# New fixed orders of TensorE, ScalarE and VectorE work in a fused attention and channel-mix kernel

## The chip, the core and the metric

The kernel runs on one core of a Trainium2 chip. The metric is the device time of one execution in microseconds (us). Five engines work side by side, each through its own list of instructions and strictly in the order of that list: TensorE (PE: matmuls and transposes; PEld is its weight loads), ScalarE (ACT), VectorE (DVE), GpSimd (POOL) and SyncE (SP). The last two mostly issue transfers (DMAs) here.

## The reference

Eight batches of eight heads; a sequence of 576 positions, 64 numbers per head. Sliding-window attention with a bias that grows with distance, and then a channel mix with a shift by one position:

```python
scores = scale * np.matmul(q, k.transpose(0, 1, 3, 2))
bias = slopes[:, None, None] * (-np.abs(rel).astype(np.float32))[None, :, :]
mask = (rel >= 0) & (rel < window)           # window = 128
...
x_prev = np.concatenate([np.zeros((B, 1, D), dtype=np.float32), x[:, :-1, :]], axis=1)
xk = mu_k * x + (1.0 - mu_k) * x_prev
xr = mu_r * x + (1.0 - mu_r) * x_prev
k = np.maximum(xk @ w_k, 0.0)
v = k * k @ w_v
r = 1.0 / (1.0 + np.exp(-(xr @ w_r)))
return (r * v).astype(np.float32)
```

Here x is the attention's output, with all heads of a position side by side (512 numbers); w_k is 512 x 1024, w_v 1024 x 512, w_r 512 x 512.

## The kernel before, in words

**Attention.** A batch is worked in four pairs of heads (g = 0 to 3). For a pair, q and k come as rows of positions and are transposed on TensorE (lines 1249 and 1252 for the first half of batch 0, line 1173 for its second half and for batches 1 and 2, line 911 for batch 3) or by transposing DMAs (batches 4 to 7); ScalarE or VectorE copies them from PSUM to tiles qk (line 759). Scores are matmuls of 64 rows, two heads at a time (line 789), ahead of which batch 0's first half gets its bias by a matmul (line 773). ScalarE takes the exponential into tiles at (line 806), VectorE multiplies by a mask (lines 815 to 827), TensorE multiplies by V, which has a column of ones (line 855, tiles vs, and tv for the last 64 positions). VectorE takes the reciprocal of the sums (line 861) and scales (line 867, tiles xu). xu is transposed to xt on TensorE (lines 894 and 911, copies on line 759) or by DMA. VectorE forms the shifted difference (line 954) and the two mixes xk and xr (line 961).

**Masks and tails.** The mask is made at the start: matmuls of line 1197, exponentials on ScalarE (line 1202), copies on VectorE (line 1215). The last 64 positions of q and k ("tails", tiles ts and tt) are transposed on lines 1015 (batch 0) and 986.

**Channel mix.** Pieces of 256, 512 and 384 positions. Eight groups of four matmuls by w_k (line 1078), each followed by a ReLU on ScalarE (line 1085) and a square on ScalarE or VectorE (lines 1057 and 1059, tiles rl to kk); per 128 positions one group by w_r (line 1096) with a tanh on ScalarE (line 1103), and two groups by w_v (line 1112). VectorE multiplies both into the output (line 1117), which SP stores (line 1142).

**Warm-up.** TensorE begins with matmuls whose result nobody reads (line 750); there are 56 of them.

**What sets the order.** Every step is a node of a plan. A table `ORDER` holds, for PE, ACT and DVE, the numbers of the nodes in the order in which that engine is to do them. A node that two engines can do (`copy_any`, `square`) is done by the engine in whose list its number stands. `Plan.run` goes through the table, follows the dependences, takes PSUM banks (eight, named p1) and tiles as they come free, and so gives each engine its list. POOL's list of loads is in the order of the code; SP's list follows from the plan. On the chip an engine waits at its next instruction until what that needs is there, and nothing behind it overtakes it (TensorE's weight loads excepted). Loads on POOL are held to eight in flight: the ninth issue waits until the first has landed.

Of the kernel before, what the change touches and what calls it, by code (L numbers as in the profile page):

```python
# [23 lines left out]
85 75 68 56 41 43 71 62 90 40 78 44 69 72 45 52 74 88 61 64 39 76 83 67 86 53 93 91 57 59 81 51 73 70 54 48 63  # L24
50 58 84 87 42 105 47 65 94 55 49 80 103 117 60 77 79 95 89 46 92 82 119 66 120 106 97 141 129 122 108 143 144
131 37 132 125 146 111 196 179 134 149 157 162 137 213 199 165 182 168 185 202 239 236 216 219 230 245 188 242
251 171 222 205 191 248 174 233 225 312 300 259 254 208 315 345 303 298 333 318 306 256 261 336 348 339 257 293
273 276 351 270 264 309 321 279 262 267 441 324 342 285 282 354 453 486 288 439 295 357 456 489 296 290 459 492
291 474 414 387 378 477 480 372 369 390 408 495 426 551 395 405 420 366 375 384 483 381 400 444 447 498 397 462
398 565 583 568 423 411 402 450 403 434 556 465 597 417 429 436 392 588 600 559 393 431 591 437 562 432 571 519  # L30
525 522 507 603 574 513 510 724 697 727 536 531 594 528 516 546 700 688 606 541 538 548 539 715 691 718 549 627
669 660 624 694 633 630 639 543 654 703 621 721 675 544 644 663 706 822 730 615 618 533 810 825 733 534 657 636
672 649 666 641 786 789 683 642 798 813 801 754 646 763 792 651 647 742 816 745 757 678 652 804 748 828 751 760
685 943 919 907 686 781 931 910 768 773 946 934 766 680 778 783 949 771 779 769 784 776 681 846 876 891 888 913
774 882 885 849 858 863 937 897 837 922 1023 834 894 879 840 1011 1026 873 843 925 868 855 1035 999 1014 852 902
860 870 865 1038 1002 866 1029 861 955 871 1017 961 964 1041 904 976 958 1005 973 984 970 994 899 967 900 905
979 989 981 1086 1101 1107 1098 1089 1053 1092 982 1050 1104 1056 1095 1047 1068 1065 986 1062 1059 1110 996 987
# [1387 lines left out]
```

## Time and profile before

| | |
|---|---|
| median of 3 runs | 231.36 us (230.56 to 231.84) |
| the profiled execution | 231.85 us, of which its span is 228.2 |
| instructions | 6317, of which 2517 matmuls |
| mean granted clock of TensorE | 0.985 |
| last matmul's end, span's end | 224.9 us, 228.2 us |

A row of a timeline reads: start, length, engine, line, operation, tile written<-tiles read, shapes, how many instructions were merged into the row and, in brackets, how long the engine stood idle before it and what ended that. Lengths of matmuls overlap, so the pace of a group is the distance from its start to the next group's start. A row of a table by stretches reads: stretch, its length, busy time (and instructions) of PE, PEld, DVE, ACT and POOL, granted clock of TensorE (1.00 is full speed), busy share of the DMA engines, GB/s.

### The profile page before, as it was taken

To read this page: it belongs to the slowest core of one execution; us is meant where nothing else is said; L and a number is where in the kernel's file an instruction comes from. 1 tells how busy PE (TensorE), PEld (TensorE's weight loads), DVE (VectorE), ACT (ScalarE), POOL (GpSimd) and SP (SyncE) were. 2 spreads that over 40 slices of the span, in tenths; PEclk is the share of its full clock that TensorE was granted. 3 is DMA by queue.
4 is the path that set the end of the run, shared out by engine and by line. 5 is a ranking of instruction groups with operands and counts; after the bars stand their busy time and mean duration, and the time that the engine had idled before them with its cause. 6 is when DMAs were issued, how large, how long until landed. Compare 5 with 4: busy or idle time off the path is not lost.

```text
span 228.2 us, 6317 instructions
## 1 busy us (share of the span) xinstructions
PE 219.5 (96%) x2517; PEld 128.7 (56%) x2517; DVE 188.5 (83%) x431; ACT 153.3 (67%) x274; POOL 92.1 (40%) x118
## 2 busy tenths in 40 slices
PE   8989889999998999999999999999999999999994
PEld 8656645845656455556665555446564554664442
DVE  6788999898768999999898978699989999854243
ACT  2897899898989875987488834933598532646111
POOL 8765557599960983347585534400000000000000
PEclk9976999999999999999999999999999999999999
DMA  6999999999999999999999999999951162120225
GB/s 166 177 187 203 193 192 179 196 181 150 182 172 151 123 170 155 194 144 159 156 193 159 171 117 184 127 233 144 261 136 30 59 138 59 47 95 0 92 92 184
DMA packets 132492, 33.96 MB, mean 149 GB/s; under 512 B 119784, under 2 KB 127984, under 8 KB 132464
## 3 DMA queue, kind: packets, MB, share of 16 engines
q0 software_dynamic: 95728, 16.26, 96.7%
q1 hardware_dynamic: 34992, 16.72, 37.5%
q10 hardware_dynamic: 1744, 0.59, 1.1%
q8 instruction: 19, 0.31, 0.5%
q14 instruction: 9, 0.07, 0.1%
HBM read 33.56 MB, written 9.44 MB: 188 GB/s over the span
## 4 chain that ended last, share of the span: by engine, by line
PE 85%; ACT 7%; DMA 3%; POOL 2%; issue 1%; DVE 0%; DVEq 0%; POOLq 0%; ACTq 0%
PE ps L1078 28%; PE ps L1112 26%; PE ps L1096 14%; PE ps L855 7%; PE ps L789 7%; DMA qx<-in_k_dram 3%; ACT qk L759 3%; ACT at L806 2%; PE ps L911 1%; ACT xt L759 1%; ACT rl L1085 1%; POOL vs L563 1%; PE ps L1173 1%; POOL qx L559 0%; PE ps L1015 0%
## 5 line engine op out<-in xcount | busy, mean ns | idle before, releaser
L1078 PE MATMUL ps<-xk,wk_sb 128*128 128x256 bf16 (+2 forms) x416 | 72.6, 318 | 0.3 <-ACT at L806 0.3
L1085 ACT ACTIVATE rl<-ps 128x256 bf16<-128x256 f32 (+2 forms) x104 | 46.9, 475 | 38.4 <-PE ps L1078 30.9
L1112 PE MATMUL ps<-wv_sb,kk 128*128 128x512 bf16 (+2 forms) x296 | 70.1, 374 | 0.0
L806 ACT ACTIVATE at<-ps 128x1024 bf16<-128x1024 f32 (+2 forms) x68 | 63.4, 987 | 5.0 <-PE ps L789 4.0
L1078 PEld LDWEIGHTS <-wk_sb 128*128 128x128 bf16 x416 | 38.4, 99 | 23.8 <-ACT rl L1085 1.2
L1112 PEld LDWEIGHTS <-kk 128*128 128x128 bf16 x296 | 26.6, 98 | 29.7 <-ACT rs L1103 1.0
L827 DVE TENSOR_TENSOR at<-at,mask 128x1024 bf16<-128x1024 bf16 x56 | 37.4, 683 | 3.3 <-ACT at L806 3.2
L563 POOL DMA_DIRECT2D vs<-in_v_dram x32 | 28.4, 895 | 24.5 <-PE ps L855 15.8
L1059 DVE TENSOR_TENSOR kk<-rl 128x256 bf16<-128x256 bf16 (+2 forms) x93 | 30.1, 335 | 8.5 <-ACT rl L1085 8.5
L1096 PE MATMUL ps<-wr_sb,xr 128*128 128x512 bf16 x144 | 36.4, 380 | 0.0
L1103 ACT ACTIVATE rs<-ps 128x512 bf16<-128x512 f32 x36 | 21.6, 612 | 21.7 <-PE ps L1096 21.7
L1117 DVE SCALAR_TENSOR_TENSOR ot<-rs,ps 128x512 f32<-128x512 bf16 (+2 forms) x37 | 24.2, 660 | 10.3 <-PE ps L1112 10.2
L867 DVE TENSOR_TENSOR xu<-ps,rc 128x640 bf16<-128x640 f32 (+2 forms) x36 | 26.5, 742 | 0.3
L961 DVE SCALAR_TENSOR_TENSOR xr<-dl,mu_sb,xt 128x576 bf16<-128x576 bf16 (+1 forms) x32 | 24.8, 777 | 0.0
L855 PEld LDWEIGHTS <-at 128*128 128x128 bf16 x576 | 21.3, 97 | 6.2 <-ACT qk L759 1.1
L961 DVE SCALAR_TENSOR_TENSOR xk<-dl,mu_sb,xt 128x576 bf16<-128x576 bf16 (+1 forms) x32 | 24.5, 777 | 0.1
L855 PE MATMUL ps<-vs,at 128*128 128x65 bf16 x512 | 22.1, 193 | 0.6 <-ACT qk L759 0.6
L594 POOL DMA_DIRECT2D cb<-in_k_dram x20 | 17.7, 908 | 9.7 <-DMA vs<-in_v_dram 6.8
L1096 PEld LDWEIGHTS <-xr 128*128 128x128 bf16 x144 | 13.0, 98 | 14.2 <-ACT rl L1085 0.7
L594 POOL DMA_DIRECT2D cb<-in_q_dram x20 | 17.7, 905 | 5.0 <-PE ps L1078 1.4
L759 ACT COPY qk<-ps 128x512 bf16<-128x512 bf16 (+1 forms) x27 | 13.6, 552 | 2.6 <-PE ps L1252 2.2
L861 DVE RECIPROCAL rc<-ps 128x10 f32<-128x10 f32 (+2 forms) x36 | 7.4, 208 | 8.9 <-PE ps L855 7.4
(83 smaller groups left out, 188.8 us busy)
## 6 DMA issues: line engine op xcount, KB each, us to landing
out_dram<-ot SPq DMA_DIRECT2D x35, 256.0 KB, 3.8
vs<-in_v_dram POOLq DMA_DIRECT2D x32, 128.0 KB, 9.0
cb<-in_q_dram POOLq DMA_DIRECT2D x20, 128.0 KB, 9.7
cb<-in_k_dram POOLq DMA_DIRECT2D x20, 128.0 KB, 7.5
wk_sb<-in_moe_w_k_dram POOLq DMA_DIRECT2D x2, 512.0 KB, 9.2
cb<-in_q_dram POOLq DMA_DIRECT2D x4, 256.0 KB, 10.0
cb<-in_k_dram POOLq DMA_DIRECT2D x4, 256.0 KB, 9.9
wv_sb<-in_moe_w_v_dram POOLq DMA_DIRECT2D x2, 512.0 KB, 11.0
```

Source lines behind the costliest of these rows:

```text
L563: return dma(POOL, 256, issue_t(1024), lambda e: nc.gpsimd.dma_start(out=vs_buf[h.idx][:, j, :, 0:D], in_=v[b, :, 128 * j:128 * j + 128].r ...
L594: return [dma(POOL, 256, issue_t(1024), lambda e, r=r: nc.gpsimd.dma_start(out=cb_buf[h.idx][:, i, r], in_=src[:, :, r]), [g], kind="q") f ...
L806: lambda e, ah=ah, w=w, hp=hp: nc.scalar.activation(out=ah(), in_=two(hp)[:, :, 0:w], func=AF.Exp, scale=float(scale)), (), [hp])
L827: nc.vector.tensor_tensor(out=a, in0=a, in1=m, op=ALU.mult)
L855: nc.tensor.matmul(a[:, hl, t - t0], lhsT=at[:, lo:lo + 128], rhs=vs[:, u, 2 * g + hl, 0:W] if u < NF else tvb[:, 2 * g + hl, 0:W], start= ...
L867: nc.vector.tensor_tensor(out=out_, in0=a5()[:, :, :, 0:D], in1=rc[:, :, 0:nt, None].to_broadcast([128, 2, nt, D]), op=ALU.mult)
L961: lambda e: nc.vector.scalar_tensor_tensor(out=buf[hk.idx][:, g, e0 + c0:e0 + c1], in0=dls(), scalar=mu[:, g:g + 1], in1=xc(1), op0=ALU.mu ...
L1059: nc.vector.tensor_tensor(out=out, in0=in_, in1=in_, op=ALU.mult)
L1078: nc.tensor.matmul(one(hp)[:, 0:n], lhsT=wk_sb[:, po, 128 * fo:128 * fo + 128], rhs=xk_buf[hx.idx][:, po, c0:c1], start=(po == 0), stop=(p ...
L1085: a = op(ACT, act_t(n), [s], pr, lambda e, hp=hp, hr=hr: nc.scalar.activation(out=rl_buf[hr.idx][:, 0:n], in_=one(hp)[:, 0:n], func=AF.Rel ...
L1096: nc.tensor.matmul(one(hp), lhsT=xr_buf[hx.idx][:, po, 128 * c:128 * c + 128], rhs=wr_sb[:, po], start=(po == 0), stop=(po == NPO - 1))
L1112: nc.tensor.matmul(one(hv)[:, a:b], lhsT=kk_buf[hk.idx][:, fo, o:o + 128], rhs=wv_sb[:, fo, a:b], start=(fo == 0), stop=(fo == NFO - 1))
```

## The change

Only the three lists in `ORDER` differ. All nodes, their code, the number of matmuls and the loads on POOL with their order are the same. The core of the diff, one line of PE's list:

```diff
 ORDER = {
     "PE": [int(x) for x in """
...
-85 75 68 56 41 43 71 62 90 40 78 44 69 72 45 52 74 88 61 64 39 76 83 67 86 53 93 91 57 59 81 51 73 70 54 48 63
...
+49 58 52 60 42 70 68 87 57 44 86 39 67 84 88 79 73 62 83 40 64 61 53 91 43 56 59 69 41 90 93 82 65 74 72 47 95
```

Sixteen nodes change their engine: nine go from VectorE to ScalarE, seven the other way (twelve of them squares, four copies). Of the warm-up matmuls 36 stay at TensorE's head, 4 stand among its first attention work, and 16 between the transposes and scores of batch 0's second half. Counted over TensorE's whole list, a 64-row matmul follows a 128-row one or the other way round 98 times, where it was 78 times. SP stores some outputs earlier or later among its transposing DMAs.

ScalarE at its start, before (after its four loads; L1202 makes a mask, qk are the transposed q and k, at the exponentials, xt the transposed output):

```order
L759 ACT_TABLE_LOAD
L759 COPY qk_72<-ps 128x2x256
L1202 ACTIVATE mask<-ps 128x4x256
L806 ACTIVATE at_77<-ps 128x2x384
L806 ACTIVATE at_78<-ps 128x2x384
L1202 ACTIVATE mask<-ps 128x4x256
L759 CAST qk_74<-ps 128x2x256
```

and now:

```order
L1202 ACT_TABLE_LOAD
L1202 ACTIVATE mask<-ps 128x4x256
L759 COPY qk_71<-ps 128x2x256
L759 COPY qk_72<-ps 128x2x256
L806 ACTIVATE at_77<-ps 128x2x384
L806 ACTIVATE at_78<-ps 128x2x384
L1202 ACTIVATE mask<-ps 128x4x256
L759 CAST qk_74<-ps 128x2x256
```

The first mask goes ahead of the first copy, and a second copy, which VectorE did, comes behind it.

TensorE where batch 0's first half is transposed (xu are the scaled outputs, at the exponentials, warm the warm-up tile), as a piece of the difference:

```order
+L894 LDWEIGHTS xu_86
+L894 MATMUL ps<-ident,xu_86 128x128
+L894 LDWEIGHTS xu_86
+L894 MATMUL ps<-ident,xu_86 128x128
+L750 LDWEIGHTS warm
+L750 MATMUL ps<-warm 128x128
 L894 LDWEIGHTS xu_85
 L894 MATMUL ps<-ident,xu_85 128x128
 L894 LDWEIGHTS xu_85
 L894 MATMUL ps<-ident,xu_85 128x128
-L855 LDWEIGHTS at_77
-L855 MATMUL ps<-vs_63,at_77 128x65
```

A warm-up matmul stands between two pairs of transposes, and the attention matmuls that stood behind the second pair have moved.

TensorE at the scores of batch 2's first two pairs of heads (tiles qk_72 and qk_73), before:

```order
L789 MATMUL ps<-qk_72 128x256
L789 LDWEIGHTS qk_72
L789 MATMUL ps<-qk_72 128x256
L789 LDWEIGHTS qk_73
L789 MATMUL ps<-qk_73 128x256
```

and now:

```order
L789 MATMUL ps<-qk_72 128x256
L789 LDWEIGHTS qk_72
L789 MATMUL ps<-qk_72 128x256
L911 LDWEIGHTS xu_85
L911 MATMUL ps<-ident,xu_85 128x64
```

The second pair's scores no longer follow the first's: twenty transposes of xu, four of the tails and two groups of w_v matmuls stand between them.

82 rows, old and new, of the table ORDER are left out of this document.

## The prediction

> **What bounds the kernel now.** I read the page first: its busy shares, its slices with the granted clock, and its chain.
>
> ```profile
> PE 219.5 (96%) x2517; PEld 128.7 (56%) x2517; DVE 188.5 (83%) x431; ACT 153.3 (67%) x274; POOL 92.1 (40%) x118
> PE   8989889999998999999999999999999999999994
> PEclk9976999999999999999999999999999999999999
> PE 85%; ACT 7%; DMA 3%; POOL 2%; issue 1%; DVE 0%; DVEq 0%; POOLq 0%; ACTq 0%
> ```
>
> TensorE carries 85% of the chain. A new order can't remove matmuls, so it can only win time in which TensorE waits, runs at a lower clock, or changes its mode. The table by stretches says where such time is (columns: PE, PEld, DVE, ACT, POOL busy, clock, DMA):
>
> ```profile
> 0.00:4.50 4.50, 3.51 (x34) 3.51 (x35) 2.52 (x21) 1.28 (x1) 3.54 (x10) 1.00 0.54 149
> 11.30:14.70 3.40, 2.70 (x104) 1.94 (x100) 2.45 (x13) 3.00 (x9) 2.70 (x4) 1.00 1.47 196
> 14.70:18.10 3.40, 2.80 (x48) 1.72 (x46) 3.40 (x13) 3.40 (x9) 1.40 (x3) 0.50 1.80 185
> 18.10:21.50 3.40, 3.23 (x22) 2.12 (x23) 2.97 (x11) 2.51 (x7) 2.15 (x4) 0.50 1.25 205
> 25.00:34.00 9.00, 7.34 (x184) 4.30 (x182) 8.54 (x21) 8.66 (x20) 5.52 (x7) 1.00 1.54 193
> 40.00:50.00 10.00, 9.47 (x248) 6.84 (x245) 9.22 (x20) 9.39 (x25) 7.48 (x10) 1.00 2.00 193
> 50.00:80.00 30.00, 29.40 (x393) 16.95 (x392) 24.93 (x52) 26.68 (x47) 21.81 (x27) 1.00 1.93 155
> 80.00:224.90 144.90, 144.88 (x1297) 79.58 (x1296) 120.21 (x247) 85.07 (x144) 36.05 (x44) 1.00 1.18 135
> ```
>
> From 80 us on TensorE is never without work: 144.88 of 144.90 us. Nothing is to be won there. What can be won lies ahead of 80 us: 6.8 us at half clock (14.7 to 21.5), 1.66 us idle between 25 and 34, 0.53 between 40 and 50, and 0.60 between 50 and 80. In the half-clock stretch, though, ScalarE and VectorE are full too (3.40 of 3.40 up to 18.1), so a full clock doesn't return the whole difference.
>
> **Part 1: the half-clock stretch.** This is what TensorE and ScalarE did around it:
>
> ```profile
> 12.43 0.38 PE L1173 MATMUL ps<-ident,qx 64*64 64x64 bf16 x24 [0.19 <-DMA qx<-in_k_dram]
> 13.29 0.65 PE L1015 MATMUL ps<-ident,ts 64*64 64x32 bf16 x32
> 14.59 0.30 PE L894 MATMUL ps<-ident,xu 128*128 128x128 bf16 x2 [0.43 <-DVE xu L867]
> 18.27 1.89 PE L1078 MATMUL ps<-xk,wk_sb 128*128 128x256 bf16 x8 [0.31 <-ACT at L806]
> 20.84 1.30 ACT L806 ACTIVATE at<-ps 128x512 bf16<-128x512 f32 x2 [0.89 <-PE ps L789]
> 23.43 0.38 ACT L1085 ACTIVATE rl<-ps 128x256 bf16<-128x256 f32 x1 [1.01 <-PE ps L1078]
> ```
>
> Ahead of the drop TensorE does small transposes with short waits between them (the longest shown is 0.43 us); the clock is halved at 14.7 and stays so for 6.8 us. The first eight channel-mix matmuls then take 1.89 us, and ScalarE waits for TensorE twice, 0.89 and 1.01 us. Those 1.90 us are what the half clock costs the engines behind it; while ScalarE was full it cost them nothing.
>
> The new order takes 20 of the 56 warm-up matmuls from the head of the program, and puts 16 of them between these transposes and the scores behind them. It also sets scores and channel-mix matmuls in turn where they stood in blocks. The price of a warm-up matmul:
>
> ```profile
> 5.31 0.50 PE L750 MATMUL ps<-warm 128*128 128x128 bf16 x6
> 5.64 0.71 PE L1252 MATMUL ps<-ident,qx 128*128 128x128 bf16 x8
> ```
>
> Six take 5.64 - 5.31 = 0.33 us, 0.055 each, so the 16 add 0.88 us of work to a stretch in which TensorE waited anyway. No row shows how much work keeps the clock up, so I bound it by two stretches. Between 11.3 and 14.7 TensorE counts as busy for 2.70 of 3.40 us (79%) and loses the clock; between 25 and 34 it is busy 7.34 of 9.00 (82%) and keeps it. With 0.88 us more in some four microseconds the first would stand above the second. I take it that the clock holds, at two chances in three.
>
> The Trainium skill, "TensorE: Matmul & The Clock Gate", section "HAM oscillation — how this bites in real kernels", says that the gate falls after an idle gap of more than about 3.4 us; this trace disagrees, since the longest gap shown there is 0.43 us. The same page of the Trainium skill, section "Part 4: PE-mode transpose", says that transposes don't count as busy in the same way; that fits the transposes ahead of the drop, and by it plain matmuls between them are the right remedy.
>
> How much can come back is bounded by the loads, which keep their order and their queue:
>
> ```profile
> 30.19 0.69 POOL L568 DMA_DIRECT2D tv<-in_v_dram x1
> tv<-in_v_dram POOLq DMA_DIRECT2D x8, 64.0 KB, 8.2
> 39.87 0.62 PE L855 MATMUL ps<-vs,at 128*128 128x65 bf16 x15
> 21.01 0.77 POOL L604 DMA_DIRECT2D wv_sb<-in_moe_w_v_dram x1 [1.25 <-DMA wk_sb<-in_moe_w_k_dram]
> wv_sb<-in_moe_w_v_dram POOLq DMA_DIRECT2D x2, 512.0 KB, 11.0
> 33.12 1.90 PE L1112 MATMUL ps<-wv_sb,kk 128*128 128x512 bf16 x8
> ```
>
> The last piece of V of the second batch lands at 30.19 + 8.2 = 38.4 us; its first attention matmul starts at 39.87, 1.5 us later. The first half of w_v lands at 21.01 + 11.0 = 32.0, and its first user starts at 33.12, 1.1 us later. Both orders have the same 585 matmuls ahead of that attention step (I counted them). So an earlier start of the steady part is worth at most 1.5 us, and the 1.9 us that ScalarE waited would be more than enough for it. The other bound is 0: these loads, or ScalarE, hold the start where it is. I take 1.0, near the upper bound, since the 1.1 us of the w_v row is the smaller slack.
>
> **Part 2: mode changes.** TensorE pays when it goes from 64-row to 128-row matmuls or back:
>
> ```profile
> 36.82 1.03 PE L1096 MATMUL ps<-wr_sb,xr 128*128 128x512 bf16 x4
> 37.69 1.04 PE L1078 MATMUL ps<-xk,wk_sb 128*128 128x256 bf16 x8
> 52.66 1.04 PE L1112 MATMUL ps<-wv_sb,kk 128*128 128x512 bf16 x4
> 53.62 0.45 PE L1173 MATMUL ps<-ident,cb 64*64 64x64 bf16 x32
> ```
>
> Four 512-wide matmuls ahead of another 128-row group take 37.69 - 36.82 = 0.87 us; ahead of a 64-row group 53.62 - 52.66 = 0.96. A change costs 0.09 us. Counted over the whole order there were 78 changes and there will be 98: 42 in place of 24 ahead of the second batch's first attention step, and 56 in place of 54 behind it. The two behind cost 2 x 0.09 = 0.2 us on the path. The 18 ahead are 1.6 us of TensorE time; I cost them at nothing, because TensorE idles 1.66 us between 25 and 34 alone and waits on loads. Without that cover they cost the 1.6.
>
> **Part 3: two stalls in the middle.**
>
> ```profile
> 48.90 0.49 PE L789 MATMUL ps<-qk 64*128 64x256 bf16 x5
> 49.89 0.39 PE L789 MATMUL ps<-qk 64*128 64x256 bf16 x3 [0.50 <-ACT xt L759]
> 73.49 0.63 PE L855 MATMUL ps<-vs,at 128*128 128x65 bf16 x15 [0.60 <-ACT qk L759]
> ```
>
> At 49.4 us the second of two score groups in a row waits 0.50 us for PSUM that ScalarE empties. In the new order the pair is parted: transposes and two groups of w_v matmuls stand between, over 2 us of work, four times the wait. That stall goes: 0.5 us. What is late next is the attention step behind it, with masks on VectorE (9.22 of 10 us busy there). The stall at 73 us (0.60) is rebuilt too, but I see no reason in the order that it should vanish or not come back elsewhere, so I count it as zero between -0.6 and +0.6.
>
> **Part 4: ScalarE's start.** ScalarE waits for its first data, then copies and makes masks:
>
> ```profile
> 6.39 0.58 ACT L759 COPY qk<-ps 128x512 bf16<-128x512 bf16 x1 [2.20 <-PE ps L1252]
> 6.99 1.02 ACT L1202 ACTIVATE mask<-ps 128x1024 bf16<-128x1024 f32 x1
> 8.38 1.04 PE L1249 MATMUL ps<-id,qx 128*128 128x128 f32 x8
> L613 ACTq DMA_DIRECT2D qx<-in_k_dram x4: 486/506/550, 0.7 to 2.3; - x4
> DMA to landing us min/median/max: 3.0/4.9/6.0
> ```
>
> The new order puts the first mask (1.02 us) ahead of the first copy, into the 2.20 us in which ScalarE waited, and takes over one copy (0.58) from VectorE: a gain of about 0.4. Against it, four of the eight float transposes of line 1249 now stand ahead of the first pair's scores and of the second mask's matmuls. Their last load is issued at 2.3 and takes up to 6.0, so it lands at about 8.3, and everything behind it on TensorE waits for that; the second exponential then starts some 0.4 later than now. I let the two cancel. Sixteen operations change between VectorE and ScalarE (nine to ScalarE, seven to VectorE, twelve of them squares); on balance that is two operations for ScalarE, which I cost at nothing, since neither engine bounds the part behind 80 us (85.07 and 120.21 of 144.90 busy).
>
> **The sum.** -1.0 (clock, up to the loads) - 0.5 (stall) + 0.2 (two mode changes) = -1.3 us. Against the profiled execution's own 231.85 us (228.2 of span and 3.65 around it) that is 230.55; against the median of the three runs, 231.36, which is 0.5 lower, it is **230.1 us**. A measurement of this kernel can tell about 0.5% (1.2 us) from no change, and the forecast lies right at that line.
>
> **The rivals.** *The loads and ScalarE hold the start.* The clock may fall again (the fillers aren't enough, or the stretch of idling around the wait for the load at 8.3 us trips it), or the gain ends at the loads. Then only parts 2 and 3 are left, -0.3: 231.1. For it: both engines are full from 14.7 to 18.1. Against: the two waits of ScalarE for TensorE.
>
> *All of the throttled time comes back.* 6.8 us at half clock are 3.4 us of lost TensorE work: 231.36 - 3.4 + 0.2 - 0.5 = 227.7. For it, TensorE is the bound. Against it, the two load rows, which allow 1.5. The Trainium skill, "TensorE: Matmul & The Clock Gate", section "Terms", prices throttled time in just this way; in this trace the engines behind TensorE were full for half of it.
>
> *Slower: the wait at 8.3 us.* TensorE is in order, so scores, second mask and fillers all wait behind the float transposes. If ScalarE then never catches up (0.4 us), and the 18 added mode changes fall on a TensorE that no longer idles (1.6), with the two behind (0.2), the time is 231.36 + 2.2 = 233.6. It decides from the point where the idle time of 1.66 us between 25 and 34 shrinks by less than the 1.6 us added. For it: that idle time is waits for ScalarE (8.66 of 9.00 busy), and ScalarE gets two more operations than it gives.
>
> **How the numbers follow.** The forecast gets 0.46, the first rival 0.20, the second 0.12, the slower one 0.22. Of the forecast's 0.46, 0.34 lie beyond the 0.5% line and 0.12 within; with the second rival that is 0.46 faster. Within: 0.12 + 0.19 = 0.31. Slower: 0.22 + 0.01 = 0.23. The range reaches to 227.8 (just short of the second rival's value) and up to 233.0, which leaves out about half of the slower rival: 227.8 to 233.0. The likeliest case's own range is 229.3 (the clock's upper bound of 1.5 and the later stall gone) to 231.0.
>
> **What would show it.** Right: the clock row without its 7 and 6 (or with a shorter dip), the first channel-mix matmul well before 18.27, the second batch's first attention step at 38.4 to 39.3 and not 39.87, and no wait of 0.5 us at its scores. Wrong: a dip in the same place; or a full clock with that attention step still at 39.9 or later, which would say that ScalarE or a load, not the clock, set the start; or new idle time between 40 and 80 us above the 1.1 us there now.

## The result, and the profile after

| | before | new |
|---|---|---|
| median | 230.96 us (230.12 to 231.88, 6 runs) | 228.84 us (226.90 to 229.21, 6 runs) |
| the profiled execution | 231.85 us, span 228.2 | 229.16 us, span 227.1 |
| mean granted clock in it | 0.985 | 0.992 |
| last matmul's end | 224.9 us | 224.0 us |

The ratio is 0.9899, with a 95% interval of [0.9867, 0.9931]: 2.3 us faster, where 1.3 were forecast. The new order was timed a second time among the experiments, with ratio 0.988 [0.9837, 0.9923].

The page of the new kernel: busy shares, TensorE's slices, the clock's slices, and the chain.

```profile
PE 217.2 (96%) x2484; PEld 127.9 (56%) x2517; DVE 188.3 (83%) x429; ACT 154.8 (68%) x276; POOL 92.4 (41%) x118
PE   8988989999999999999999999999999999999994
PEclk9997999999999999999999999999999999999999
PE 86%; DVE 6%; ACT 4%; issue 3%; DVEq 0%; ACTq 0%
```

The clock's row has a 7 where it had 7 and 6. Of 2517 matmuls 2484 have a record, while all 2517 weight loads (PEld) do. So gaps of 0.16 us ahead of groups "x3" below are a missing matmul, not a wait, and where I compare progress I go by the weight loads. The table by stretches (columns as before):

```profile
11.30:14.70 3.40, 3.06 (x91) 2.14 (x95) 2.80 (x13) 2.60 (x6) 2.96 (x4) 1.00 1.44 197
14.70:18.10 3.40, 2.35 (x73) 1.67 (x73) 3.40 (x13) 2.44 (x8) 1.45 (x3) 1.00 1.86 181
18.10:21.50 3.40, 3.13 (x37) 1.55 (x31) 2.50 (x9) 3.37 (x7) 2.02 (x4) 0.72 1.26 209
21.50:25.00 3.50, 3.50 (x50) 2.65 (x49) 2.18 (x9) 2.62 (x6) 1.00 (x2) 0.79 1.41 194
25.00:34.00 9.00, 7.87 (x209) 4.97 (x209) 8.54 (x24) 8.11 (x18) 5.70 (x7) 1.00 1.52 194
```

The half clock no longer covers 14.7 to 21.5. It now falls between 18.1 and 25.0, and is half as long: a clock of 0.72 over 3.4 us and 0.79 over 3.5 is (0.28 x 3.40 + 0.21 x 3.50) x 2 = 3.4 us at half speed, where it was 6.8. TensorE's timeline of the new kernel:

```profile
17.58 0.32 PE L1173 MATMUL ps<-ident,qx 64*64 64x64 bf16 x15 [1.05 <-issue]
19.14 0.65 PE L1078 MATMUL ps<-xk,wk_sb 128*128 128x256 bf16 x4 [0.21 <-ACT at L806]
31.99 0.33 PE L986 MATMUL ps<-ident,ts 128*128 128x128 bf16 x3 [0.53 <-issue]
40.81 0.62 PE L855 MATMUL ps<-vs,at 128*128 128x65 bf16 x15
49.46 0.39 PE L789 MATMUL ps<-qk 64*128 64x256 bf16 x4
52.13 0.39 PE L789 MATMUL ps<-qk 64*128 64x256 bf16 x4
73.96 0.62 PE L855 MATMUL ps<-vs,at 128*128 128x65 bf16 x15
```

The first channel-mix matmul starts at 19.14 where it was 18.27, and the second batch's first attention step at 40.81 where it was 39.87. So the new start is not earlier. By these two executions it is 0.9 us later, but single executions scatter by more than that: with lists that are the same up to there, the attention step stands at 39.87, 40.34 and 41.41 with the old start (before, and x1 and x6 of the experiments below), and at 40.81, 40.97 and 40.41 with the new one (new, x12 and x2). The two waits in the middle (0.50 at 49.4 us, 0.60 at 73 us) are gone: the parted score groups at 49.46 and 52.13 and the attention step at 73.96 have no bracket behind them. New are two waits "<-issue", 1.05 and 0.53 us, in which the profile shows nothing that TensorE waits for.

How far each kernel is at equal work, in us behind the kernel before (minus: ahead). I take the matmul work that stands ahead of each weight load and compare the starts of the weight loads at the same amount of it; the first column is the time at which the kernel before has done it. Orders differ, so single values are good to some 0.3. The last three columns are for experiments below.

| before, us | new | old start, new rest (x1) | new with 8 changes fewer (x10) | new from 40 to 77 us only (x5) |
|---|---|---|---|---|
| 10.25 | +0.5 | +0.2 | +0.4 | -0.1 |
| 21.9 | +1.4 | +0.4 | -0.1 | 0.0 |
| 41.0 | +0.9 | +0.4 | -0.1 | +1.1 |
| 47.6 | +1.1 | +0.9 | 0.0 | +0.9 |
| 50.7 | +0.3 | +0.2 | -0.8 | +0.1 |
| 70.5 | -0.2 | -0.3 | -1.3 | -0.4 |
| 81.6 | -0.1 | -0.2 | -1.2 | +1.2 |
| 103.2 | -1.0 | -1.1 | -2.1 | +1.2 |
| 223.6 | -1.1 | -1.2 | -2.1 | +1.2 |

The new kernel loses 1.4 us up to 22 us, gets 0.8 back at the stall at 49 us and 0.5 more up to 70 us, and the rest after that. How matmuls are weighted matters in the rows between 70 and 104 us. With each kind counted at the pace it keeps behind 40 us (the mean from one start to the next), the new kernel stands at 0.0 at 70.5, -0.4 at 81.6 and -0.7 at 103.2: then 0.4 comes where the wait of 73 us was, and 0.6 behind 81.6. (The other 1.6 us by which the two profiled executions differ lie outside the span, 3.65 and 2.06 us; over the 32 runs of before beside x1 that part is 2.1 us in the mean, so the execution of before that was profiled lay high in it.)

Each timed run lists its mean granted clock, and the values come in three groups: up to 0.988 (nearly all of them 0.982 to 0.985), 0.990 to 0.993, and 0.998 to 1.000. By the profiled executions these are 6.8, 3.4 and 0 us at half speed (in x3's the 6.8 are two stretches of 3.4, the second from 31.8 us on). That gives a second way to part the gain (only the executions that the ratios use are counted, the new order's from both times it was run and the kernel before's from all; this leaves out one of the new order, 231.14 us at a clock of 0.986):

| at half speed | before: runs, mean us | new: runs, mean us |
|---|---|---|
| 6.8 us | 58, 231.21 | 0 |
| 3.4 us | 25, 230.28 | 4, 229.05 |
| none | 10, 229.96 | 7, 228.06 |
| all | 93, 230.82 | 11, 228.42 |

With the new order's shares of the groups the kernel before would take (4 x 230.28 + 7 x 229.96) / 11 = 230.08. So of the 2.4 us, 0.7 go with a shorter half-clock stretch and 1.7 with the order at equal clock. In the kernel before itself the executions without half clock are 1.25 us faster than those with 6.8 us of it.

### The profile page after: what moved, and what is told of

Its sections match the earlier page's. It is cut to its first block, busy times and chain, and to the rows that moved or that the text cites. A ratio compares the mean times of both kernels' runs of the same rounds, so it can differ in the third digit from the quotient of the medians.

```text
span 227.1 us, 6305 instructions
## 1 busy us (share of the span) xinstructions
PE 217.2 (96%) x2484; PEld 127.9 (56%) x2517; DVE 188.3 (83%) x429; ACT 154.8 (68%) x276; POOL 92.4 (41%) x118
## 4 chain that ended last, share of the span: by engine, by line
PE 86%; DVE 6%; ACT 4%; issue 3%; DVEq 0%; ACTq 0%
PE ps L1112 26%; PE ps L1078 25%; PE ps L1096 13%; PE ps L789 7%; PE ps L855 6%; PE ps L750 2%; ACT at L806 2%; DVE xu L867 2%; PE ps L1173 2%; DVE ot L1117 1%; PE ps L911 1%; ACT mask L1202 1%; DVE at L827 1%; DVE xr L961 1%; DVE kk L1059 1%
## 5 line engine op out<-in xcount | busy, mean ns | idle before, releaser
L1078 PE MATMUL ps<-xk,wk_sb 128*128 128x256 bf16 (+2 forms) x409 | 70.9, 316 | 0.7 <-ACT at L806 0.2
L1112 PE MATMUL ps<-wv_sb,kk 128*128 128x512 bf16 (+2 forms) x289 | 68.8, 374 | 0.5 <-issue 0.2
L806 ACT ACTIVATE at<-ps 128x1024 bf16<-128x1024 f32 (+1 forms) x68 | 64.1, 985 | 4.6 <-PE ps L789 4.6
L1078 PEld LDWEIGHTS <-wk_sb 128*128 128x128 bf16 x416 | 37.6, 98 | 23.8 <-ACT rl L1085 2.8
L827 DVE TENSOR_TENSOR at<-at,mask 128x1024 bf16<-128x1024 bf16 x56 | 36.7, 682 | 4.5 <-ACT at L806 4.5
L1096 PE MATMUL ps<-wr_sb,xr 128*128 128x512 bf16 x125 | 33.0, 379 | 1.6 <-issue 0.6
L1096 PEld LDWEIGHTS <-xr 128*128 128x128 bf16 x144 | 13.1, 98 | 13.6 <-ACT rl L1085 0.3
L759 ACT COPY qk<-ps 128x512 bf16<-128x512 bf16 (+1 forms) x29 | 14.9, 551 | 1.7 <-PE ps L1173 1.4
```

Of the source, the lines that this page charges most:

```text
L806: lambda e, ah=ah, w=w, hp=hp: nc.scalar.activation(out=ah(), in_=two(hp)[:, :, 0:w], func=AF.Exp, scale=float(scale)), (), [hp])
L827: nc.vector.tensor_tensor(out=a, in0=a, in1=m, op=ALU.mult)
L1078: nc.tensor.matmul(one(hp)[:, 0:n], lhsT=wk_sb[:, po, 128 * fo:128 * fo + 128], rhs=xk_buf[hx.idx][:, po, c0:c1], start=(po == 0), stop=(p ...
L1096: nc.tensor.matmul(one(hp), lhsT=xr_buf[hx.idx][:, po, 128 * c:128 * c + 128], rhs=wr_sb[:, po], start=(po == 0), stop=(po == NPO - 1))
L1112: nc.tensor.matmul(one(hv)[:, a:b], lhsT=kk_buf[hk.idx][:, fo, o:o + 128], rhs=wv_sb[:, fo, a:b], start=(fo == 0), stop=(fo == NFO - 1))
```

## The experiments

All use the same nodes and code; only the lists differ. But the plan gives out the PSUM banks by its own reckoning of time, so an edited list also moves banks: against the order that each edit started from, 54 of the plan's 322 takings of banks differ in x3, 89 in x4, 105 in x7, 97 in x8, 42 in x10 and 67 in x11.

### The two halves: x1 and x2

The cut lies behind 131 of the 418 numbers of TensorE's list (the second batch's first attention step), where both orders have done the same nodes. x1 has the old start and the new rest, x2 the new start and the old rest. TensorE's list of x1 against the new kernel's:

```diff
...
-257 293 351 270 264 276 273 321 309 262 279 267 441
+257 293 273 276 351 270 264 321 309 262 279 267 441
...
```

> The order of before up to the second batch's first attention step, the new order behind it. If the clock at the start made the gain (the prediction's part 1), this loses most of it: 0.5 to 0.7 us faster than before (ratio 0.997 to 0.998). If the gain comes from behind 45 us and the new start costs about 1 us (what the two traces seem to say), it is 2.5 to 3.5 us faster than before (ratio 0.985 to 0.989), at least as good as the whole change, with that attention step back near 39.9 us.

> The mirror image: the new order up to the second batch's first attention step, the old one behind it. Clock theory: 1 to 1.5 us faster than before (ratio 0.993 to 0.996). Other theory: the start is about 1 us later and nothing makes up for it, 0.5 to 1.5 us slower than before (ratio 1.002 to 1.006), with that attention step near 40.8 us.

Measured: x1 229.42 us, ratio 0.9928 [0.9891, 0.9964]; x2 231.28 us, ratio 1.0021 [0.9988, 1.0054]. The rest alone carries 1.7 us, the start alone nothing. The two waits in the middle are gone in x1 (TensorE's timeline):

```profile
45.77 0.60 PE L855 MATMUL ps<-vs,at 128*128 128x65 bf16 x14 [0.43 <-ACT xt L759]
49.33 0.39 PE L789 MATMUL ps<-qk 64*128 64x256 bf16 x4
52.00 0.39 PE L789 MATMUL ps<-qk 64*128 64x256 bf16 x4
```

and its stretch from 50 to 80 us:

```profile
50.00:80.00 30.00, 30.00 (x408) 17.89 (x407) 25.41 (x52) 29.27 (x54) 21.85 (x27) 1.00 1.91 156
```

TensorE is busy for all of 50 to 80 us, where it idled 0.60 before. A new wait of 0.43 stands at 45.77, at the seam of the two orders. So the gain behind 40 us is shown, and it is not the clock's. The halves don't add up: -1.7 and +0.5 make -1.2, and the whole gives -2.3. Each half is uncertain by 0.8 us either way, so that this difference is not clear of the noise. At equal half-clock time x2 is slower than the kernel before, by 0.6 us (230.55 against 229.96, none) and 1.5 us (231.77 against 230.28, 3.4 us): the new start loses elsewhere what its shorter half-clock stretch brings.

### The warm-up matmuls between the transposes: x3 and x4

x3 is the new order with its 20 moved warm-up matmuls back at the head (which also leaves 90 changes between 64 and 128 rows in place of 98). x4 is the old order with 16 of its warm-up matmuls put between the transposes of batch 0's second half:

```diff
...
-125 146 111 196 179 134 149 157 162 137 213 199 165
+125 85 146 111 75 196 68 56 41 179 43 49 80 134 60 149 77 157 162 79 89 46 137 92 82 213 66 199 165
...
```

> The new order with its 20 moved warm-up matmuls back at the head of TensorE's list; nothing else changes. If the fillers hold the clock, the half-clock stretch grows back to two windows of 3.4 us and the time rises by 1 to 1.7 us over the new kernel (ratio to before 0.994 to 0.998). If they do nothing for the time, it is within 0.4 us of the new kernel (ratio 0.988 to 0.992), whatever the clock row shows.

> The old order with 16 warm-up matmuls put between the transposes of batch 0's second half, nothing else changed. Clock theory: the granted clock loses at most one window and the time falls by 0.7 to 1.5 us (ratio 0.994 to 0.997). If ScalarE, VectorE and the loads set the start, the clock row may be full and the time is within 0.4 us of before (ratio 0.998 to 1.002).

Measured: x3 228.29 us, ratio 0.9914 [0.9877, 0.995]; x4 231.2 us, ratio 1.001 [0.9975, 1.0044]. With or without them no difference is clear of the uncertainty, in either order. But the half clock does answer to them. Counted over the executions that the ratios use, as groups of 6.8, 3.4 and 0 us at half speed:

| | 6.8 us | 3.4 us | none |
|---|---|---|---|
| old start, all warm-ups at the head (before, x1, x5, x6, x9) | 84 | 34 | 16 |
| old start with 16 between (x4) | 2 | 7 | 2 |
| new start, all at the head (x3, x11) | 5 | 13 | 3 |
| new start with 16 between (new, x2, x7, x10) | 1 | 20 | 24 |

So they do shorten the stretch: 6.8 us stand in 84 of 134 executions of the old start without them and in 2 of 11 with them, in 5 of 21 of the new start without them and in 1 of 45 with them (with every execution counted 88 of 138, 3 of 12, 5 of 21 and 3 of 48). A good part comes with the rest of the new start, since its 5 of 21 are without any moved warm-up matmul. And something else eats the gain. TensorE's timeline of x3, of x4 and of x2:

```profile
16.93 0.23 PE L789 MATMUL ps<-qk 64*128 64x128 bf16 x2 [0.41 <-ACT at L806]
17.97 0.86 PE L1078 MATMUL ps<-xk,wk_sb 128*128 128x256 bf16 x4 [0.22 <-ACT at L806]
31.35 0.33 PE L986 MATMUL ps<-ident,ts 128*128 128x128 bf16 x3 [1.21 <-issue]
```

```profile
16.90 0.28 PE L1173 MATMUL ps<-ident,qx 64*64 64x64 bf16 x10 [0.53 <-issue]
20.04 1.89 PE L1078 MATMUL ps<-xk,wk_sb 128*128 128x256 bf16 x8 [0.31 <-ACT at L806]
```

```profile
17.34 0.34 PE L1173 MATMUL ps<-ident,qx 64*64 64x64 bf16 x15 [1.01 <-issue]
31.59 0.33 PE L986 MATMUL ps<-ident,ts 128*128 128x128 bf16 x3 [0.82 <-issue]
```

With the warm-up matmuls between the transposes (new, x2, x4) a wait "<-issue" of 0.5 to 1.05 us stands at 17 us; without them (x3) there is none. The last section says what it goes with. In x4 the first channel-mix matmuls come at 20.04, 1.8 us later than before, and still run at half speed (1.89 us for eight).

### Eighteen mode changes more: x8

The old order, with nine warm-up matmuls put one by one between nodes of 64-row matmuls. That is 96 changes in place of 78, and 9 x 0.055 = 0.5 us of matmul work in the stretch.

```diff
...
-196 179 134 149 157 162 137 213 199 165 182 168 185 202 239 236 216
+196 80 179 134 149 157 60 162 137 213 77 199 79 165 89 182 46 168 92 185 82 202 239 236 216
...
```

> The order of the kernel before, with nine of its warm-up matmuls (128 rows) taken from the head and put one by one between two nodes of 64-row matmuls, from 12.5 to 20 us. That adds 18 changes between 64 and 128 rows (96 in all, the new order has 98) and 0.5 us of matmul work. If changes are covered by idle time at the start, as the prediction costed them, the time is that of the run with 16 warm-up matmuls and only four more changes, ratio 1.001. If they are not covered, 18 x 0.09 = 1.6 us come on top: ratio 1.006 to 1.008. The half-clock stretch may end earlier or later in single runs; runs are compared at equal clock as well.

Measured: 232.98 us, ratio 1.0097 [1.0059, 1.0134], 2.2 us slower. At equal half-clock time (6.8 us) it is 232.94 against 231.21, 1.7 us, with one execution at a clock of 0.978 (some 10 us at half speed) left aside. Both are near the uncovered price, 18 x 0.09 + 0.5 = 2.1. But the changes are not all that differs. Ahead of the first added change, TensorE waits for ScalarE's second mask in x8, which it doesn't in the kernel before (TensorE's row, then ScalarE's):

```profile
10.91 0.50 PE L773 MATMUL ps<-dist,sid 128*128 128x384 bf16 x2 [0.47 <-ACT mask L1202]
9.80 1.06 ACT L1202 ACTIVATE mask<-ps 128x1024 bf16<-128x1024 f32 x1
```

In x8's plan the matmuls of 10.91 write banks 2 and 3, which that mask still reads; in the plan of before they write 0 and 1. By equal work this execution of x8 is 1.1 us behind at 10.25 us already, where no change is added yet, 2.5 behind at 18.3 us, and stays there to the end. So some 1.4 us of its delay stand where the changes are, and the idle time behind them did not take that back; how much of the 2.2 us is the changes' alone, x8 doesn't show.

### Fewer changes in the new order: x10 and x11

x10 moves eight nodes of the new order so that 64-row matmuls stand together: 90 changes. x11 has all warm-up matmuls at the head and three scores moved: 84 changes. In x11 the plan's figure for the time in which it reckons TensorE cold (`COLD`) is changed, so that all PSUM banks behind 47 us come out as in the new kernel; in x10 they do so by themselves.

```diff
...
-162 46 81 137 199 54 80 45 85 213 182 202 55 165 185 239 168 230 216 236 219
+162 46 81 54 80 45 85 55 137 199 213 182 202 165 185 168 239 230 216 219 236
...
```

and in x11, beside its list:

```diff
-    COLD = 5.6
+    COLD = 3.85
```

> The new order with eight nodes of TensorE's list moved between 15 and 22 us so that 64-row matmuls stand together: five warm-up matmuls go ahead of the transposes of xu, two groups of scores change places with channel-mix groups. 90 changes between 64 and 128 rows in place of 98; all lists of the other engines and all PSUM banks behind 47 us are those of the new kernel. If the changes at the start are on the path (as the run with 18 more changes in the old order says), it gains 8 x 0.09 = 0.7 us on the new kernel: 228.1 us, ratio to the kernel before 0.986 to 0.987. If they are covered at this place by ScalarE's and VectorE's work, the time is that of the new kernel, ratio 0.990.

> The new order with all 56 warm-up matmuls at TensorE's head and three moves of scores, so that it has 84 changes between 64 and 128 rows in place of 98; the plan's figure for the warm-up time is set so that all banks behind 47 us come out as in the new kernel. Theory (changes on the path, and the fillers only shorten the half-clock stretch while they bring a later instruction fetch): 14 x 0.09 = 1.3 us gained by the changes, up to 1.2 by the missing wait for the fetch at 17 us, and up to 1 lost where the stretch at half clock is longer: 227.5 to 228.5 us, ratio 0.984 to 0.988. Rival (the prediction's part 1: the warm-up matmuls between the transposes hold the clock, and that is worth about 1 us): it is 1 us slower than the new kernel, ratio 0.994.

Measured: x10 229.52 us, ratio 0.9947 [0.9914, 0.9979]; x11 229.42 us, ratio 0.9952 [0.9922, 0.9982]. Both expectations of a gain fail: neither is faster than the new order, and by their middle values they are 0.5% slower. x10's profiled execution, without any half clock, shows one reason why a faster start doesn't come through (TensorE's timeline, and ScalarE's exponential ahead of the second wait's end):

```profile
17.05 0.32 PE L1173 MATMUL ps<-ident,qx 64*64 64x64 bf16 x16 [0.82 <-issue]
30.91 0.40 PE L986 MATMUL ps<-ident,ts 128*128 128x128 bf16 x4 [1.10 <-ACT at L806]
29.14 1.08 ACT L806 ACTIVATE at<-ps 128x1024 bf16<-128x1024 f32 x1
```

and its stretch from 25 to 34 us:

```profile
25.00:34.00 9.00, 7.42 (x190) 4.34 (x189) 8.41 (x21) 8.40 (x19) 5.70 (x7) 1.00 1.53 193
```

Further ahead at 22 us than the new kernel, TensorE then waits 1.10 us ahead of 30.91, and idles 1.58 us between 25 and 34 (1.13 in the new kernel). The bracket names an exponential, but none ends there: the one of 29.14 is done at 30.22, 0.7 us before TensorE goes on, and the next one at 31.14. x11 has the same wait, with 0.8 us between the exponential's end and TensorE's start:

```profile
31.95 0.40 PE L986 MATMUL ps<-ident,ts 128*128 128x128 bf16 x4 [1.22 <-ACT at L806]
30.08 1.08 ACT L806 ACTIVATE at<-ps 128x1024 bf16<-128x1024 f32 x1
```

In TensorE's list both stand where new, x2, x3, x7 and x12 have their second wait "<-issue" (last section). So it is most likely the same wait, for instructions, and not one for ScalarE. That explains a gain of nothing; it doesn't explain a loss, since this execution (228.00 us, the lowest of x10's) is no slower than the new order's without half clock (228.06 in the mean). The loss in the median stays open.

### The float transposes later: x7

The new order, with the four float transposes of the fourth pair (node 141) behind the second mask's matmuls (node 97), as in the kernel before.

```diff
...
-120 141 106 94 97 129 143
+120 106 94 97 141 129 143
...
```

> The new order with one node of TensorE's list moved: the four float transposes of the fourth pair of heads (line 1249) stand behind the second mask's matmuls again, and no longer ahead of the scores of the first pairs. My prediction's part 4: the wait for their load at about 8 us then stops nothing but themselves, the second exponential of ScalarE starts 0.4 us earlier, and all that follows does, so the kernel is 0.4 us faster than the new one: 228.1 to 228.4 us, ratio to the kernel before 0.988. Rival: the start is held by something else (loads, ScalarE's own work, the later instruction fetch), and the time is that of the new kernel, ratio 0.990. Third: TensorE sits idle one load longer and is behind by the length of these transposes, 0.8 us, ratio 0.993.

Measured: 229.4 us, ratio 0.9947 [0.9919, 0.9974]. The third case's number came out, but not for its reason. At 10 us the trace is 0.15 us ahead of the new kernel's, and stays within 0.2 of it up to 70 us; so by these two executions the wait at 8 us cost about 0.2, not 0.4; a difference of that size between single executions is not clear of their scatter. The loss is at 75 us. TensorE of x7, and then ScalarE:

```profile
72.88 1.04 PE L1112 MATMUL ps<-wv_sb,kk 128*128 128x512 bf16 x4
74.96 0.63 PE L855 MATMUL ps<-vs,at 128*128 128x65 bf16 x15 [1.05 <-ACT at L806]
```

```profile
73.82 1.08 ACT L806 ACTIVATE at<-ps 128x1024 bf16<-128x1024 f32 x1
```

The lists of TensorE and ScalarE are the new kernel's there, and yet the attention step waits 1.05 us until the exponential of 73.82 ends at 74.90. The new kernel has the same step at 73.96 without a wait. What differs is a number that no list shows: in the plan of x7 the step writes PSUM banks 0 and 1, which that exponential still reads, and in the new kernel's banks 2 and 3. The exponential writes another tile (at_78) than the step reads (at_77), so that it is not the data that the step waits for. The plan gives out banks by its own reckoning of when they are free, and one node moved at 8 us has them given out in another order from then on. I did not run x7 with the new kernel's banks, so that the bank makes the wait is read from the plan and the two rows, and not shown by an edit.

### Pieces of the rest: x5, x6 and x9

x5 is the old order with only the piece from 40 to 77 us new (66 numbers of TensorE's list), x9 with only the piece from 40 to 54 us (25 numbers), x6 with only the part behind 77 us. The piece of x9, which parts the pair at 49 us:

```diff
...
-309 321 279 262 267 441 324 342 285 282 354 453 486 288 439 295 357 456 489 296 290 459 492 291 474
+321 309 262 279 267 441 324 342 285 354 282 486 453 288 295 489 357 439 296 290 456 474 291 492 459
...
```

> The order of the kernel before everywhere except for one piece: the 66 nodes of TensorE's list that stand from the second batch's first attention work (about 40 us) to about 77 us, with the ScalarE and VectorE work that belongs to them, are in the new order (50 of these nodes change their place). Theory A (two stalls): what the new order gains behind 40 us are the two waits of 0.50 and 0.60 us for PSUM that the kernel before has at 49.4 and 73.5 us, and both lie in this piece: all of the gain of the run with the old start and the new rest (1.7 us) is here, ratio to the kernel before 0.993 to 0.995, and neither wait is in the trace. Theory B (it comes bit by bit, all along the order): about half, ratio 0.997. Theory C (a stall comes back right behind the piece, because the old order behind it expects its work at the old time): ratio 0.999 to 1.001.

> The order of the kernel before up to about 77 us, and the new one behind it (196 nodes of TensorE's list change their place). My prediction had it that nothing is to be won there, since TensorE is busy for 144.88 of 144.90 us behind 80 us in the kernel before. By that and by theory A (two stalls) the ratio is 1.000. By theory B (bit by bit) it is 0.996 to 0.997, since the two traces drift apart by about 0.6 us behind 80 us.

> The order of the kernel before everywhere, but with the 25 nodes of TensorE's list between about 40 and 54 us (18 of them change their place), and the ScalarE and VectorE work that belongs to them, in the new order: the pair of score groups at 49.4 us is parted, and nothing else is done. By part 3 of the prediction the wait of 0.50 us goes and the kernel gains 0.5 us: ratio 0.998, and the trace is 0.5 us ahead at 54 us. Rival (seams): at the place where the old order goes on, work waits that the new order had not made ready, as in the run with 40 to 77 us new; then the trace is ahead at 54 us and behind again by 80 us, ratio 1.002 to 1.006.

Measured: x5 231.75 us, ratio 1.0056 [1.0021, 1.0091]; x6 233.58 us, 1.0122 [1.0081, 1.0164]; x9 231.96 us, 1.0054 [1.0021, 1.0087]. All three are slower, so the expectations from theories A and B fail as times. The traces say why. TensorE's waits behind 40 us in x5, in x9 and in x6 (all of 0.4 us and more up to 100 us):

```profile
41.50 0.63 PE L855 MATMUL ps<-vs,at 128*128 128x65 bf16 x15 [0.60 <-ACT rl L1085]
80.64 0.34 PE L789 MATMUL ps<-qk 64*128 64x256 bf16 x4 [0.40 <-ACT at L806]
81.55 0.34 PE L789 MATMUL ps<-qk 64*128 64x256 bf16 x4 [0.52 <-ACT at L806]
```

```profile
41.49 0.63 PE L855 MATMUL ps<-vs,at 128*128 128x65 bf16 x15 [0.60 <-ACT rl L1085]
55.18 1.91 PE L1078 MATMUL ps<-xk,wk_sb 128*128 128x256 bf16 x12 [0.97 <-DVE qk L759]
74.59 0.60 PE L855 MATMUL ps<-vs,at 128*128 128x65 bf16 x14 [0.57 <-ACT qk L759]
```

```profile
51.43 0.39 PE L789 MATMUL ps<-qk 64*128 64x256 bf16 x3 [0.49 <-ACT xt L759]
75.03 0.63 PE L855 MATMUL ps<-vs,at 128*128 128x65 bf16 x15 [0.60 <-ACT qk L759]
79.38 1.04 PE L1096 MATMUL ps<-wr_sb,xr 128*128 128x512 bf16 x4 [0.52 <-ACT rl L1085]
84.90 0.34 PE L789 MATMUL ps<-qk 64*128 64x256 bf16 x4 [0.80 <-ACT at L806]
96.81 0.63 PE L855 MATMUL ps<-vs,at 128*128 128x65 bf16 x15 [0.41 <-ACT xt L759]
```

Where a piece is new, its old wait is gone: x9 lost the one at 49 us and kept the one at 74.59, x5 lost both (but for 0.3 us inside the step at 73.76, which takes 0.89 us and not 0.62), x6 kept both. And at each seam stands a new wait: 0.60 on the way in, 0.97 (x9) or 0.40 and 0.52 (x5) on the way out, 0.52 and 0.80 (x6). In the table of progress x5 starts its piece 1.1 us behind, is at -0.4 by 70 us, and is at +1.2 behind the exit. So the two waits are worth what theory A says (1.1 us of waits, 1.5 us of progress inside the piece), and a piece of an order taken by itself pays it back at its ends. x6 can't say what the part behind 77 us is worth by itself: its seam hides it. Nor is all of its loss the seam's. Its profiled execution ends 3.2 us behind the kernel before, but 1.5 of them stand there by 25 us, where its lists are those of the kernel before: the first row of ScalarE comes 1.1 us later than the 6.39 of before.

```profile
7.47 0.59 ACT L759 COPY qk<-ps 128x512 bf16<-128x512 bf16 x1 [3.29 <-PE ps L1252]
```

So two executions of the same start can differ by more than a microsecond, and what single traces differ by at the start says little.

### The new order again: x12

> The new order itself, unedited, with more executions. Four edits of its start (float transposes later, 8 changes fewer, 14 changes fewer with all warm-up matmuls at the head, warm-up matmuls at the head alone) gave ratios of 0.9947, 0.9947, 0.9952 and 0.9914, all above the 0.9899 that six executions of the new order gave. If each of these edits really costs up to 1.1 us, the new order gives 0.990 again (228.4 to 228.9 us). If the edits are worth nothing that can be measured and six executions happened to lie low, it gives 0.993 to 0.995 (229.1 to 229.6 us). By theory A (two stalls and little else) about 1.1 + 0.3 - 0.5 = 0.9 us come from behind 40 us net of the later start, 0.996.

Measured: 228.61 us, ratio 0.988 [0.9837, 0.9923]. The first of the two cases: the six executions had not happened to lie low. No run of the study beats the new order by more than the uncertainty (x3 comes nearest, at 0.9914).

## Why the prediction was right or wrong

**The number.** 230.1 us was forecast, 1.3 below the kernel before; 2.3 us were measured, and 228.84 lies inside the range of 227.8 to 233.0, though just below the likeliest case. (Its lower end was given as 229.3; with its own terms, 1.5 for the clock and 0.6 for the later stall, it is 231.36 - 1.5 - 0.5 + 0.2 - 0.6 = 229.0.) The sign was right. The way there was right in one part of three, and it is luck that the total came out inside: a start that gained nothing was made up for by two gains that the sum held at nothing.

**Part 1, the half-clock stretch (-1.0).** Half of the mechanism is there. Warm-up matmuls between the transposes do shorten the stretch (2 of 11 executions with 6.8 us in place of 84 of 134 in the old start, 1 of 45 in place of 5 of 21 in the new one), and a full clock is worth about what was taken for it: 1.25 us lie between the executions of the kernel before with 6.8 us at half speed and with none, and 0.7 of that is what the new order's executions come to. The step that failed is the next one, that the steady part would then start earlier, "at 38.4 to 39.3 and not 39.87": in none of the traces with the new start is it ahead of 39.81 (x10), and in the new kernel it is 40.81, which the prediction had put down as the sign that the clock does not set the start. The forecast took the loads for the bound on what can come back, and had no term for a wait that neither list shows: TensorE stands 1.05 us at 17.6 and 0.53 at 32.0 for what are most likely its own instructions, and 1.10 and 1.22 us at the second of these places in x10 and x11. The start by itself (x2) then gains nothing, with a ratio of 1.0021.

**Part 2, the changes of mode (18 ahead at nothing, +0.2 behind).** The price of a change was right: behind 81 us the trace of the kernel before has 32 changes, and each lengthens the distance to the next matmul's start by 0.092 to 0.096 us. Whether the 18 ahead are covered is not settled. In the old order, x8 loses 2.2 us with 18 changes, 0.5 us of matmuls and a moved bank. In the new order taking 8 or 14 of them away (x10, x11) gains nothing, while the wait at 31 us grows. By the prediction's own test the idle time between 25 and 34 us should have shrunk by 1.6 us, and it shrank from 1.66 to 1.13; but 0.53 of the 1.13 is the new wait "<-issue", and the rest shrank by 1.1. "Costed at nothing" was a guess that the new order doesn't contradict, and no rule.

**Part 3, the stalls.** The wait of 0.50 us at 49.4 went as forecast, for the reason given: two groups of w_v matmuls and twenty transposes now stand between the two score groups. Progress there is 0.8 us. The other wait was counted as zero between -0.6 and +0.6, and came out at its lower end: it is gone and came back nowhere in the new kernel. That term was mis-sized by 0.6. I saw no cause in the order that it should vanish, and the cause is not in the order of work but in the banks. ScalarE in the kernel before, and then in the new one, ahead of the attention step (73.49 and 73.96):

```profile
72.81 0.62 ACT L759 COPY qk<-ps 128x512 bf16<-128x512 bf16 x1
```

```profile
73.29 0.41 ACT L1085 ACTIVATE rl<-ps 128x256 bf16<-128x256 f32 x1
```

In the plan of before the step writes banks 4 and 5, and that copy reads bank 4: it ends at 73.43, and the step starts at 73.49. It is so in x2, x6 and x9, which have the wait too: there a copy to qk from one of the step's two banks ends 0.05 to 0.06 us before TensorE goes on. In the new kernel the step writes banks 2 and 3, and bank 3 is read by the ReLU of 73.29; that ends at 73.70, and the step starts at 73.96 without a wait, as in x1. So six traces agree with their plans; no run changes the bank alone.

**Part 4, ScalarE's start (0).** The first mask does start earlier, 5.91 in place of 6.99, and the first two exponentials end later (8.23 + 1.60 = 9.83 us against 9.42 before). ScalarE in the new kernel and then in the kernel before:

```profile
5.91 1.02 ACT L1202 ACTIVATE mask<-ps 128x1024 bf16<-128x1024 f32 x1 [1.72 <-PE ps L1197]
8.23 1.60 ACT L806 ACTIVATE at<-ps 128x768 bf16<-128x768 f32 x2
```

```profile
7.91 1.51 ACT L806 ACTIVATE at<-ps 128x768 bf16<-128x768 f32 x2
```

At 10 us the kernel is 0.5 behind, and x7 puts 0.2 on the wait for the float transposes, which was priced at 0.4. Both are within what two executions of one start differ by (1.1 us between before and x6 at the same copy), so whether the two effects cancel, as forecast, is not shown.

**Behind 80 us (nothing).** "Nothing is to be won there" was too strong. Between 81.6 and the end the new kernel and x1 gain 0.6 to 1.0 us by equal work, as the matmuls are weighted, with some 0.3 of uncertainty, without a wait of TensorE in x1. I have no experiment that parts it from the rest, and so what it is stays open. With the wait at 73 us it is what makes the kernel faster than forecast.

**The rivals.** "The loads and ScalarE hold the start" has the outcome of the start, which gains nothing, but not the cause that the traces show: the waits that stand there are most likely for instructions, and neither loads nor ScalarE. It failed on the sum, since it had only 0.5 of the gain in the middle. "All of the throttled time comes back" would have needed 3.4 us from the clock; 0.7 came, and executions of the kernel before without any half clock are only 1.25 us faster than those with 6.8 us of it. The slower rival's mechanism, mode changes on a TensorE that no longer idles, may stand behind a part of x8's loss, and did not decide this kernel.

The Trainium skill, "TensorE: Matmul & The Clock Gate", section "What's actually happening", says that the gate looks at a free-running window of some 3.4 us. The runs agree with that better than with a fixed place: the stretches at half speed are 3.4 or 6.8 us long (18.1 to 25.0 holds 3.4 us here), the stretches at full speed ahead of them and behind them are whole multiples of 3.41 us (10.24, 13.65, 204.8 and 208.2 us), and the same kernel has none, one or two windows at half speed from run to run (10, 25 and 58 of 93). So "the clock holds" is not a yes or no of an order; an order sets how often it does.

## What to carry to other kernels

An order of work is worth what it is worth as a whole: a better piece put into an old order lost its gain at the seams (0.6 to 1.3 us of waits each), and moving one early node, which gave the PSUM banks out in another order, went with a new wait of 1.05 us more than 60 us later. So look for gains of a new order at the waits that the trace names in the steady part, and weigh each of them, also those for which no reason is seen. When a resource such as a bank is given out by a planner, compare what it gave out before and after: that is where the second stall went. And a bracket that names an engine is to be held against the time at which that engine was done: the wait at 31 us that looks like ScalarE's ended 0.7 us later than the work it names.

## What the runs showed of the hardware

**TensorE stands still at fixed places of its list, most likely for its own instructions.** The two waits "<-issue" stand ahead of a weight load that waits for no semaphore. They are at the 222nd and the 476th weight load of TensorE's list, 254 apart, in the new kernel, x2 and x12; x7 has them at the 223rd and the 476th, x3 only the second, x10 only the first, and x4 one at the 224th. Counted over TensorE's whole list with its semaphore instructions, they are at place 442 or 443 and at place 954 or 955, some 512 apart, whatever work stands there. The waits of x10 and x11 at 31 us, which the profile puts down to an exponential, are at place 954 too. On the queue of kind "instruction" (19 packets of 16 KB in the execution) one packet starts ahead of each such place. The table of transfers, kind, packets, MB and share, of the new kernel between 15.0 and 16.2 us and of the kernel before between 12.0 and 13.1 us:

```profile
q8 instruction: 1, 0.02, 5.1%
```

Both read alike; what differs is the time. In the new kernel the packet starts at 15.1 us and the 222nd weight load at 17.58, 2.5 us later, 1.26 us after the load ahead of it. In the kernel before and in x3 the packet starts at 12.1 and 12.3, and the load comes at 14.93 and 15.93, without such a wait. With 16 warm-up matmuls between the transposes (or beside them, in x10) the packet starts at 14.6 to 15.5 (new, x2, x4, x7, x10, x12), without them at 12.1 to 12.9 (the eight others). Why it starts later there the traces don't show; that the wait goes with the later start is all that is shown. For the place at 31 us there is more. The third packet starts in all fourteen traces when TensorE has begun its 427th to 434th weight load, and the load at that place comes 2.3 to 2.8 us behind the packet's start: 2.35 to 2.61 in the seven traces that wait there (new, x2, x3, x7, x10, x11, x12), and 2.39, just without a wait, in the kernel before. So a start that does this piece of the list faster has to wait at its end. No run moves a packet by itself.

**A change between 64-row and 128-row matmuls costs TensorE 0.09 us.** Behind 81 us, where TensorE never waits, 32 changes of the kernel before lengthen the distance between two starts by 0.092 to 0.096 us each. What they cost where TensorE waits anyway is not shown: x8's 2.2 us for eighteen changes and nine matmuls hold a wait for a moved bank too.
